# A graph aggregation kernel: the run gathers, the leftover gathers and the start of the last merge block are put at other places in the program

## The chip, the core and the metric

One core of one Trainium2 chip runs the whole kernel. The metric is the device time of one execution in microseconds. Before the change it is 1911.4 us, the median of three runs (1903.02, 1911.40 and 1920.62).

## The reference

Every one of 12500 nodes adds up the feature rows of its neighbours over 800000 edges, scales the sum and applies two small weight matrices.

```
N, deg, D = 12500, 64, 64
E = N * deg
def reference(x, src, dst, deg_inv, w_self, w_neigh):
    nsum = _segment_sum(x[src], dst, N)
    h_neigh = nsum * deg_inv[:, None]
    return x @ w_self + h_neigh @ w_neigh
```

`src` and `dst` are drawn at random, so what is costly is the gather `x[src]` and the sum by `dst`.

## The kernel before

**Sorting.** Each edge becomes a key that holds its bucket: 78 groups of 160 destination nodes, times 98 blocks of 128 source nodes, which is 7644 buckets of some 105 edges. VectorE sorts 128 rows of 6250 keys each by compare and exchange (lines L229). The sorted rows are then cut into pieces ("runs") so that one partition gets a run from every row, and the runs of one partition are merged. This is done in two parts: part 0 holds buckets 0 to 4735 (128 partitions of 37), part 1 the rest (128 of 23). GpSimd (POOL) fetches the runs with one indirect DMA for each of the 128 runs of a part (`gather_runs`, line L393), and after each of them writes a small tile once or twice (`pause`, L306). VectorE merges them (`merge_runs`, L415 for the first step of a block of runs and L455 for the others).

**Windows.** In the merged rows each bucket has a window. A count over the row finds where it begins, and POOL fetches it with an indirect DMA (`find_and_gather`, tile `v`, L605). The windows of part 0 come in two halves: the lower buckets, whose rows are merged first, and the upper ones. `decode_buckets` takes the windows apart: destination numbers are turned on TensorE and kept in `dlT`, source numbers go to DRAM as `sl`. Edges that do not fit a window become "leftovers" (`leftovers`), 64 columns of up to 128 edges for each part.

**Sums.** `nodes` walks over the buckets in tiles of eight: 956 tiles, numbered from 0. For each group of 28 buckets (three and a half tiles) SyncE loads `slb`, and VectorE makes the one-hot matrices `ohs` (L823) and `ohd` (L826); there are three buffers for `ohs`, so VectorE can be about ten tiles ahead. For each tile TensorE multiplies the one-hots with the node features (L852 into `ct`, eight matmuls), ScalarE copies `ct` to `xg` (L862), and TensorE adds `xg` times `ohd` into the sums `acc` (L907, sixteen matmuls). Six groups of destinations share one pair of accumulators, so a stretch ends after 588 buckets, which is 73.5 tiles. ("Octet" is the code's word for such a stretch: `OCT`.)

**Leftovers in the sums.** `uses` gives every leftover column the bucket number from which it may be added: the moment of its use. `rest` is called at every tile. At most five columns ahead of use it lets POOL gather the 128 feature rows of a column by an indirect DMA (tile `lx`, L871), then VectorE makes its one-hot (`ohl`, L879), and at the use TensorE multiplies the two (L887). TensorE takes its instructions in order, so it stands still at L887 until the gather has landed.

**Who sets the order.** The order on each engine is written out by hand (`manual_schedule`): the merge of part 1 is a generator from which some steps are taken at every tile. Its first block (runs 0 to 63) runs beside the windows of part 0; its second block (64 to 95) from tile 8 on; its third block (96 to 127) and all that follows from tile `RESUME` on. POOL's run gathers for part 1 stand in three places: 64 behind the row search, 32 behind the upper windows, and the last 32, one at each odd tile, from tile 1 to tile 63. POOL, like every engine, works its instructions off in order.

Of the kernel before, what the change touches and what calls it, by code (L numbers as in the profile page):

```python
# [22 lines left out]
NB = 98  # L23
# [21 lines left out]
EDGE = 32  # L45
PAUSE = (1, 2)
FIRST = 64
THEN = 96
EXT = 31
SIDE = H + EXT  # L50
# [3 lines left out]
BIG = float(np.array(BIGBITS, np.uint32).view(np.float32))  # L54
SIG = 5.5
AHEAD = 44
RESUME = 80
PACE = 420
SHARE = 503
SHARED = 60  # L60
# [9 lines left out]
OCT = 6  # L70
# [190 lines left out]
class Kernel:  # L261
# [533 lines left out]
    def uses(self):  # L795


        out = []
        for o in range(0, NBID, OCT * NB):
            end = min(o + OCT * NB, NBID)  # L800
            here = []
            for p in range(2):
                for c in range(64):
                    lo = max(o, BASE[p] + c * 2 * KPRS[p])
                    hi = min(end, BASE[p] + (c + 1) * 2 * KPRS[p])
                    if hi > lo:
                        here.append([max(hi + 56, 380 + 24 * c) if p == 0 else hi + 56, p, c, lo // NB, (hi - 1) // NB])
            at = end + 8
            for use in sorted(here)[::-1]:
                at = use[0] = min(use[0], at - 24)  # L810
            out += sorted(here)
        return out
# [16 lines left out]
    def nodes(self, pool, aps, mps):  # L829
# [34 lines left out]

        def rest(b0):

            if len(picked) < self.used + 5 and len(picked) < len(uses) and uses[len(picked)][0] - 160 <= b0 \
                    and uses[len(picked)][1] in self.left:
                _, p, c, _, _ = uses[len(picked)]
                x = pool.tile([128, 128], FH, name="lx", bufs=5)  # L870
                nc.gpsimd.indirect_dma_start(  # L871
                    out=x, out_offset=None, in_=self.xt,
                    in_offset=bass.IndirectOffsetOnAxis(ap=self.left[p][1][:, c:c + 1], axis=0))
                picked.append(x)
                self.picked = len(done)
            if len(ohl) < len(picked) and len(ohl) < self.used + 5 and uses[len(ohl)][0] - 96 <= b0:
                _, p, c, first, end = uses[len(ohl)]
                m = pool.tile([128, 4 * HN], FH, name="ohl", bufs=5)
                nc.vector.tensor_scalar(m[:, :(end + 1 - first) * 2 * HN], self.wide[:, :(end + 1 - first) * 2 * HN],  # L879
                                        self.left[p][0][:, c:c + 1], -float(first * 2 * HN),  # L880
                                        op0=OP.subtract, op1=OP.is_equal)
                ohl.append(m)
            while self.used < len(uses) and uses[self.used][0] <= b0:
                _, p, c, first, end = uses[self.used]
                m = ohl[self.used].rearrange("p (b h n) -> p b h n", h=2, n=HN)
                for h in range(2):
                    nc.tensor.matmul(acc[h][:, first % OCT * HN:(first % OCT + end + 1 - first) * HN],  # L887
                                     picked[self.used], m[:, :end + 1 - first, h], start=False, stop=False)
                self.used += 1
# [167 lines left out]
    def after_sort(self, es, mps, aps):  # L1057
        tc = self.tc
        l2, l2b, l2a, va = ExitStack(), ExitStack(), ExitStack(), ExitStack()
        self.merged = self.lower = False  # L1060


        with tc.manual_schedule():
            low, middle, high = self.segments
            sync = tc.nc.sync
            for step in low:
                step()
            sync.dma_start(self.d1[0][:, :SPLITS[0]], self.runs[:, :SPLITS[0]])
            rows = self.find_rows(0, mps)
            n = 0  # L1070
            for i, step in enumerate(middle):
                step()
                while n < NEARLY * (i + 1) // len(middle):
                    n = next(rows) + 1
            sync.dma_start(self.d1[0][:, SPLITS[0]:SPLITS[1]], self.runs[:, SPLITS[0]:SPLITS[1]])
            u1, other, u0 = [stack.enter_context(tc.tile_pool(name=f"l2{i}", bufs=1))
                             .tile([128, 2 * EDGE + 128 * WIDE[p]], F32, name="u")
                             for i, (stack, p) in enumerate(((l2, 1), (l2b, 0), (l2a, 0)))]
            for u in (u1, other, u0):
                tc.nc.gpsimd.memset(u[:, :EDGE], 0.0)  # L1080
            for _ in rows:
                pass
            self.gather_runs(0, u0, range(128))
            for step in high:
                step()
            sync.dma_start(self.d1[1], self.runs[:, UPPER1:])
            self.l1ab.close()
            rows = self.find_rows(1, mps)
            for _ in range(SHARED):
                next(rows)  # L1090
            ways = None
            for i, _ in enumerate(self.merge_runs(0, u0, other, ((0, 2), (2, 1), (3, 1)))):
                if rows and [next(rows, None) for _ in range(2 - i % 2)][-1] is None:
                    rows = None
                    self.l1b.close()
                    self.gather_runs(1, u1, range(FIRST))
                    dl = es.enter_context(tc.tile_pool(name="dl", bufs=1, side="right"))
                    self.dlT = dl.tile([128, NCOL], BF, name="dlT")
                if self.lower and not ways:
                    vp = va.enter_context(tc.tile_pool(name="va", bufs=1, side="right"))  # L1100
                    self.windows(0, vp)
                    self.store_rows(0, sync)
                    ways = self.find_and_gather(0, range(NLOWER), 1)
                elif ways and i % 2:
                    next(ways, None)
            for _ in ways:
                pass
            self.store_rows(1, sync)
            self.sums_and_merge(es, mps, aps, u1, other, l2, l2b, l2a, va, vp)

    def sums_and_merge(self, es, mps, aps, u1, other, l2, l2b, l2a, va, vp):
# [11 lines left out]
        for slot in range(at[-1] + 2):  # L1123
            t += SLOT
            if ways and next(ways, None) is None:
                ways = None
                self.gather_runs(1, u1, range(FIRST, THEN))
            if slot < KPRS[0] - NLOWER and not on_act2(0, NLOWER + slot):
                t -= 750
            if slot in at or slot - 1 in at:  # L1130
                next(decode)
                t -= 1175
            while t > 0 and steps < per:
                t -= next(merge)
                steps += 1
# [11 lines left out]
        for n in self.nodes(fin, aps, mps):  # L1147
            if left and n >= left_at:
                wait = next(left, None)
                if wait is None:  # L1150
                    left = None
                    if 1 in self.left:
                        self.check(fin, mps)
                else:
                    left_at = n + wait
            if runs and n % 2:
                self.gather_runs(1, u1, [runs.pop(0)])
            if tail and n % 2:
                next(tail, None)
            if merge and n >= 8 and (n >= RESUME or steps < 2 * per):  # L1160
                t += PACE
                while merge and t > 0:
                    dt = next(merge, None)
                    steps += 1
                    if dt is None:
                        merge = None
                        self.merged = True
                        assert self.rows is u1
                        l2b.close()
                        vp = vb.enter_context(tc.tile_pool(name="vb", bufs=1))  # L1170
                        self.windows(1, vp)
                        self.store_rows(2, tc.nc.scalar)
                        find = self.find_and_gather(1, range(KPRS[1]), LAG)
                    else:
                        t -= dt
            elif find:
                if n % 2 == 0 and self.picked < n - 1 and next(find, None) is None:
                    find = None
                    decode = self.decode_buckets(1, self.v, vp, mps)
                    tail = self.tail(mps)  # L1180
            elif decode:
                if next(decode, None) is None:
                    assert n < 128 * KPRS[0] // 8 - 12
                    decode = None
                    left, left_at = self.leftovers(1, mps), 0
# [29 lines left out]
```

## Time and profile before

| what | value |
|---|---|
| median of three runs | 1911.4 us |
| time of the profiled execution | 1896.69 us |
| its span, first to last instruction | 1895.0 us |
| VectorE (DVE) busy | 1677.9 us, 89% |
| ScalarE (ACT) busy | 1166.8 us, 62% |
| TensorE (PE) busy | 962.2 us, 51% |
| GpSimd (POOL) busy | 841.8 us, 44% |
| mean granted TensorE clock | 0.793 |

The shares are averages over stages that have different limits: the first 800 us sort and merge on VectorE, with TensorE almost idle, and the sums fill the rest. So the table only says where to look; what a change in one stage is worth has to be read from that stage.

### The profile page before, as it was taken

The page shows a single profiled execution, that of the slowest core. Times are in us where ns is not written, and L with a number is a line of the kernel's source. Part 1 is how long each engine was busy: PE and PEld are TensorE (multiplying, and loading weights), DVE is VectorE, ACT ScalarE, POOL GpSimd, SP SyncE. Part 2 cuts the span into 40 slices and gives each one's busy share as a digit, 9 for nine tenths or more (in the row PEclk, how much of TensorE's full clock was granted, in tenths as well). Part 3 has the DMA queues.
Part 4 walks back from the last instruction along what each step waited for, and adds up shares of the span by engine and source line. Part 5 has one row for each costly group of instructions (what it writes and reads, how often), then busy time and mean ns, then how long its engine had stood idle before and what let it go on. Part 6 is the DMA issues. An engine that isn't in the chain of part 4 may idle for free.

```text
span 1895.0 us, 54521 instructions
## 1 busy us (share of the span) xinstructions
PE 962.2 (51%) x23659; PEld 838.7 (44%) x23659; DVE 1677.9 (89%) x1778; ACT 1166.8 (62%) x1835; POOL 841.8 (44%) x917
## 2 busy tenths in 40 slices
PE   0033000000000000083788887988979999889987
PEld 0023000000000000073677776777768788778886
DVE  7999999997749999795699999998998898888885
ACT  7463019305510022574689888988988887788786
POOL 1000000599889984798737322204662232322421
PEclk9985555555555555587899999999999999999998
DMA  4322000001100012274577877779867888888874
GB/s 152 70 63 73 0 24 8 25 20 52 22 20 10 10 38 70 82 283 137 185 230 246 256 244 251 251 258 312 285 223 250 270 276 257 269 272 278 272 252 147
DMA packets 104804, 305.24 MB, mean 161 GB/s; under 512 B 52945, under 2 KB 60491, under 8 KB 103915
## 3 DMA queue, kind: packets, MB, share of 16 engines
q1 hardware_dynamic: 86347, 277.44, 41.5%
q0 software_dynamic: 17632, 22.17, 8.7%
q8 instruction: 187, 3.06, 0.6%
q10 hardware_dynamic: 576, 2.07, 0.3%
q14 instruction: 62, 0.51, 0.1%
HBM read 282.20 MB, written 19.41 MB: 159 GB/s over the span
## 4 chain that ended last, share of the span: by engine, by line
DVE 40%; PE 24%; POOL 18%; issue 11%; DMA 3%; ACT 3%; DVEq 0%; SPq 0%; ACTq 0%; POOLq 0%
DVE u L455 14%; PE ct L852 13%; POOL u L393 13%; PE acc L907 9%; DVE a L229 7%; DVE b L229 7%; DVE ohd L826 5%; DVE ohs L823 4%; POOL pad L306 3%; POOL lx L871 2%; ACT xg L862 2%; DMA slb<-sl 1%; PE po L970 1%; DMA rd<-dst 1%; PE acc L887 1%
## 5 line engine op out<-in xcount | busy, mean ns | idle before, releaser
L862 ACT ACTIVATE xg<-ct 128x1024 f16<-128x1024 f32 (+1 forms) x898 | 856.4, 1043 | 188.6 <-PE ct L852 167.1
L852 PE MATMUL ct<-xh,ohs 128*128 128x128 f16 x7644 | 540.3, 224 | 69.7 <-DVE ohs L823 36.2
L852 PEld LDWEIGHTS <-ohs 128*128 128x128 f16 x7644 | 449.4, 100 | 110.0 <-issue 51.3
L393 POOL DMA_INDIRECT u<-d,ix x256 | 369.4, 1443 | 217.0 <-DVE ix L385 175.3
L907 PE MATMUL acc<-ohd,xg 64*128 64x80 f16 x15288 | 399.9, 200 | 58.9 <-issue 40.5
L455 DVE TENSOR_TENSOR u<-u 128x1456 f32<-128x1456 f32 (+46 forms) x292 | 394.5, 1378 | 6.6
L871 POOL DMA_INDIRECT lx<-xt,lsrc x140 | 265.6, 1897 | 249.1 <-PE acc L887 213.1
L907 PEld LDWEIGHTS <-xg 64*128 64x128 f16 x15288 | 318.4, 96 | 126.2 <-issue 57.4
L826 DVE TENSOR_TENSOR ohd<-iota,dlT 128x2240 f16<-128x2240 bf16 x273 | 360.3, 1320 | 0.0
L823 DVE TENSOR_SCALAR ohs<-slb,pidx 128x3584 f16<-128x3584 bf16 x273 | 314.6, 1152 | 37.4 <-PE ct L852 25.7
L383 PE MATMUL stp<-idf,st 128*128 128x128 f32 x2 | 0.9, 446 | 356.7 <-DVE st L381 356.7
L229 DVE TENSOR_TENSOR a<-b 128x608 f32<-128x608 f32 (+44 forms) x124 | 173.9, 1445 | 4.6
L229 DVE TENSOR_TENSOR b<-a 128x608 f32<-128x608 f32 (+44 forms) x124 | 173.9, 1444 | 4.3
L978 POOL DMA_DIRECT2D out<-o x25 | 22.8, 913 | 319.7 <-DVE o L977 245.5
L383 PEld LDWEIGHTS stp<-idf,st 128*128 128x128 f32 x2 | 0.4, 182 | 357.2 <-issue 357.2
L662 PE MATMUL tr<-idb,l 128*128 128x128 bf16 x60 | 8.0, 273 | 262.2 <-ACT l L656 258.1
L860 DVE CAST xg<-ct 128x1024 f16<-128x1024 f32 x64 | 78.3, 1223 | 57.6 <-PE ct L852 57.1
L662 PEld LDWEIGHTS <-l 128*128 128x128 bf16 x60 | 5.0, 117 | 265.5 <-ACT l L656 260.8
L420 ACT ACTIVATE u<-u 128x30 f32<-128x30 f32 (+34 forms) x136 | 30.7, 278 | 134.8 <-DVE u L455 73.0
L231 ACT ACTIVATE b<-a 128x1 f32<-128x1 f32 (+21 forms) x52 | 18.7, 379 | 135.5 <-DVE a L229 130.4
L605 POOL DMA_INDIRECT v<-d,ix x60 | 75.4, 1257 | 59.6 <-ACT ix L623 47.4
L374 ACT ACTIVATE junka<-b,c 128x132 bf16<-128x132 f32 (+46 forms) x205 | 90.6, 442 | 11.8 <-DVE b L229 5.9
(153 smaller groups left out, 798.6 us busy)
## 6 DMA issues: line engine op xcount, KB each, us to landing
slb<-sl SPq DMA_DIRECT2D x273, 896.0 KB
u<-d,ix POOLq DMA_INDIRECT x256
xt<-xh SPq DMA_DIRECT2D x1, 3136.0 KB
fo<-own SPq DMA_DIRECT2D x26, 120.0 KB
own<-os SPq DMA_DIRECT2D x12, 256.0 KB
out<-o POOLq DMA_DIRECT2D x24, 120.0 KB
lx<-xt,lsrc POOLq DMA_INDIRECT x140
rd<-dst SPq DMA_DIRECT2D x4, 521.0 KB
```

Source lines behind the costliest of these rows:

```text
L229: nc.vector.tensor_tensor(view(dst, lo + sh, [[st, g], [1, l]]), x, y, op=op)
L374: nc.scalar.activation(junks[0][:, :n], w, AF.Sign, bias=self.c1[:, 0, c:c + 1], accum_out=a)
L393: nc.gpsimd.indirect_dma_start(out=u[:nr, EDGE + p * w:EDGE + (p + 1) * w], out_offset=None, in_=src, in_offset=bass.IndirectOffsetOnAxis( ...
L455: nc.vector.tensor_tensor(view(dst, EDGE + o + out, d), view(src, EDGE + o + x, d), view(src, EDGE + o + x + gap, d), op=op)
L605: self.nc.gpsimd.indirect_dma_start(out=self.v[:, k].bitcast(F32), out_offset=None, in_=flat(self.d2[home(part, k)], 128 * PITCH2[home(par ...
L823: nc.vector.tensor_scalar(s.rearrange("p c s -> p (c s)"), b, self.pidx[:, :1], None, op0=OP.is_equal)
L826: nc.vector.tensor_tensor(d, self.iota[:, None].to_broadcast([128, 14, HN, 2]), ix, op=OP.is_equal)
L852: nc.tensor.matmul(ct[:, i * 128:(i + 1) * 128], cols[i][0], self.xh[:, (b0 + i) % NB].rearrange("p a f -> p (a f)"), start=True, stop=True)
L860: nc.vector.tensor_copy(xg[:, :cnt * 128], ct[:, :cnt * 128])
L862: nc.scalar.activation(xg[:, :cnt * 128], ct[:, :cnt * 128], AF.Copy)
L871: nc.gpsimd.indirect_dma_start(out=x, out_offset=None, in_=self.xt, in_offset=bass.IndirectOffsetOnAxis(ap=self.left[p][1][:, c:c + 1], ax ...
L907: nc.tensor.matmul(acc[h][:, db % OCT * HN:(db % OCT + 1) * HN], xg[r, i * 128:(i + 1) * 128], d[r], start=db % OCT == 0 and sb == 0, stop ...
```

## The change

Five numbers or rules are changed. The amount of work stays the same: 128 run gathers for part 1, 140 leftover gathers, the same merge steps.

1. Runs 64 to 70 of part 1 are gathered behind the windows of the lower buckets, ahead of the upper windows, and no longer behind them (`MORE = 71`).
2. The last 32 runs are issued at every third tile, from tile 0 to tile 93.
3. The third block of the merge begins at tile 100, not 80 (`RESUME`).
4. In the first stretch the eight leftover columns are all due at its end, 24 buckets apart: from bucket 404 on (404, 428, ..., 572), where the old rule set the first at 380.
5. In that stretch a column's gather may be issued up to 400 buckets ahead of its use, and no longer 160.

```
-RESUME = 80
+MORE = 71
+RESUME = 100
 ...
-                        here.append([max(hi + 56, 380 + 24 * c) if p == 0 else hi + 56, p, c, lo // NB, (hi - 1) // NB])
+                        here.append([end if o == 0 else hi + 56, p, c, lo // NB, (hi - 1) // NB])
 ...
-            if len(picked) < self.used + 5 and len(picked) < len(uses) and uses[len(picked)][0] - 160 <= b0 \
+            early = 400 if b0 < OCT * NB - 160 else 160
+            if len(picked) < self.used + 5 and len(picked) < len(uses) and uses[len(picked)][0] - early <= b0 \
 ...
+            self.gather_runs(1, u1, range(FIRST, MORE))
             self.store_rows(1, sync)
 ...
-                self.gather_runs(1, u1, range(FIRST, THEN))
+                self.gather_runs(1, u1, range(MORE, THEN))
 ...
-            if runs and n % 2:
+            if runs and n % 3 == 0:
                 self.gather_runs(1, u1, [runs.pop(0)])
```

**POOL, between the lower and the upper windows of part 0.** `v` are window gathers (18 lower, 19 upper), `u` a run gather of part 1, `pad` its pause. Before:

```order
L393 DMA u<-d_1_61,ix_1468 128x48
L306 MEMSET pad 128x95 x2
L605 DMA v<-d_0_64,ix_0_1803 128x190 x18
L605 DMA v<-d_1_65,ix_0_1803 128x190 x19
L393 DMA u<-d_1_61,ix_1468 128x48
L306 MEMSET pad 128x95 x2
```

After:

```order
L606 DMA v<-d_0_64,ix_0_1803 128x190 x18
L394 DMA u<-d_1_61,ix_1468 128x48
L307 MEMSET pad 128x95 x2
...
L606 DMA v<-d_1_65,ix_0_1803 128x190 x19
L394 DMA u<-d_1_61,ix_1468 128x48
L307 MEMSET pad 128x95 x2
```

Seven of the pairs `u`, `pad` now stand between the two groups of windows (the pairs left out at the dots are the other six).

**POOL, in the first stretch of the sums.** `lx` is a leftover gather. Before, the first one stands behind 47 run gathers that follow the upper windows, and the next ones are mixed with run gathers:

```order
L871 DMA lx<-xt,lsrc_2726 128x128
L393 DMA u<-d_1_61,ix_1468 128x48
L306 MEMSET pad 128x95 x2
L871 DMA lx<-xt,lsrc_2726 128x128
L393 DMA u<-d_1_61,ix_1468 128x48
L306 MEMSET pad 128x95 x2
L393 DMA u<-d_1_61,ix_1468 128x48
```

After, five of them stand close together behind 30 run gathers, and the sixth and seventh behind twelve more:

```order
L873 DMA lx<-xt,lsrc_2723 128x128 x2
L394 DMA u<-d_1_61,ix_1468 128x48
L307 MEMSET pad 128x95 x2
L873 DMA lx<-xt,lsrc_2723 128x128 x2
L394 DMA u<-d_1_61,ix_1468 128x48
L307 MEMSET pad 128x95 x2
L873 DMA lx<-xt,lsrc_2723 128x128
L394 DMA u<-d_1_61,ix_1468 128x48
L307 MEMSET pad 128x95 x2
...
L873 DMA lx<-xt,lsrc_2723 128x128 x2
```

So the first five columns are issued 17 run gathers sooner, while the sixth column (due at bucket 524) has 44 run gathers and five `lx` ahead of it. Behind it come two run gathers, two `lx`, four runs, `lx`, three runs, `lx`, two runs, an output, a run, `lx`, and run 127, the last.

**VectorE, where the third block of the merge begins.** `u<-u` with 16x41 is the first step of the block. Before, it follows the second block at once:

```order
L455 TENSOR_TENSOR u<-u 128x441
L455 TENSOR_TENSOR u<-u 128x429
L415 TENSOR_TENSOR u<-u 128x16x41
L823 TENSOR_SCALAR ohs<-slb,pidx 128x3584
L826 TENSOR_TENSOR ohd<-iota,dlT 128x2240
L415 TENSOR_TENSOR u<-u 128x16x41
```

After, only one-hots stand ahead of it:

```order
L881 TENSOR_SCALAR ohl<-wide,lp_2721 128x320
L824 TENSOR_SCALAR ohs<-slb,pidx 128x3584
L827 TENSOR_TENSOR ohd<-iota,dlT 128x2240
...
L416 TENSOR_TENSOR u<-u 128x16x41
L881 TENSOR_SCALAR ohl<-wide,lp_2721 128x320
L416 TENSOR_TENSOR u<-u 128x16x41
```

Counted in groups of one-hots, the block's first step has moved from behind the 26th to behind the 31st, which is from tile 84 to tile 100, and the steps after it, the search of the windows of part 1 and their decoding by four groups, 14 tiles.

## The prediction

> **What bounds the kernel now.** I read the busy times by slice first:
>
> ```profile
> span 1895.0 us, 54521 instructions
> PE   0033000000000000083788887988979999889987
> DVE  7999999997749999795699999998998898888885
> ```
>
> A slice is 47.4 us. The sums begin in the 18th; in the next one and the one after TensorE (PE) falls to 3 and 7, and VectorE (DVE) to 5 and 6: something holds up both. PE's waits name it (time in all, times, longest):
>
> ```profile
> PE acc L887 <- DMA lx<-xt,lsrc: 37.6, 4, 26.5
> ```
>
> Next PE's timeline (start, duration; in brackets the idle time before and its releaser), then DVE's:
>
> ```profile
> 891.13 0.32 PE L887 MATMUL acc<-ohl,lx 128*128 128x80 f16 x2 [26.53 <-DMA lx<-xt,lsrc]
> 903.30 0.45 PE L887 MATMUL acc<-ohl,lx 128*128 128x160 f16 x2 [5.03 <-DMA lx<-xt,lsrc]
> 919.46 0.45 PE L887 MATMUL acc<-ohl,lx 128*128 128x160 f16 x2 [5.83 <-DMA lx<-xt,lsrc]
> 891.48 0.30 DVE L879 TENSOR_SCALAR ohl<-wide,lp 128x320 f16<-128x320 f16 x1 [21.43 <-PE acc L887]
> 906.78 1.15 DVE L823 TENSOR_SCALAR ohs<-slb,pidx 128x3584 f16<-128x3584 bf16 x1 [6.00 <-PE ct L852]
> 921.56 1.39 DVE L823 TENSOR_SCALAR ohs<-slb,pidx 128x3584 f16<-128x3584 bf16 x1 [6.96 <-PE ct L852]
> 941.68 1.39 DVE L415 TENSOR_TENSOR u<-u 128x656 f32<-128x656 f32 x1 [1.09 <-issue]
> ```
>
> PE waits for the first leftover column from 864.6 to 891.1, and twice again; DVE runs its buffers full and stops too. The last row is the third merge block. POOL's timeline shows why `lx` is late:
>
> ```profile
> 733.34 0.95 POOL L605 DMA_INDIRECT v<-d,ix  x1 [0.30 <-issue]
> 753.63 0.98 POOL L605 DMA_INDIRECT v<-d,ix  x1 [19.34 <-ACT ix L623]
> 785.76 0.94 POOL L393 DMA_INDIRECT u<-d,ix  x1 [0.30 <-issue]
> 834.55 2.94 POOL L393 DMA_INDIRECT u<-d,ix  x1 [0.15 <-issue]
> 838.07 2.92 POOL L393 DMA_INDIRECT u<-d,ix  x1 [0.16 <-issue]
> 856.65 1.35 POOL L393 DMA_INDIRECT u<-d,ix  x1 [0.15 <-issue]
> 871.62 0.95 POOL L393 DMA_INDIRECT u<-d,ix  x1 [0.15 <-issue]
> 887.74 0.95 POOL L871 DMA_INDIRECT lx<-xt,lsrc  x1 [0.96 <-issue]
> 935.18 1.63 POOL L393 DMA_INDIRECT u<-d,ix  x1 [0.30 <-issue]
> ```
>
> From 785.76 on POOL has no idle time to speak of. Its run gathers (L393 by window, count in brackets) set the pace:
>
> ```profile
> 640.00:703.00 63.00, 49.02 (x25) 0.50 0.08 23
> 830.00:853.00 23.00, 18.93 (x8) 1.00 0.72 258
> 853.00:870.00 17.00, 12.44 (x8) 0.92 0.73 259
> 870.00:887.00 17.00, 10.44 (x11) 0.50 0.14 40
> ```
>
> With its pause, a gather takes 2.9 us, then 2.1, and 1.55 while DVE stands still. So POOL is the bound up to 935.18, where run 127 is issued and the third block may follow. After it DVE is full for 346 us, up to the last merge step, and then the sums run at the pace of PE and ScalarE. Busy times of all engines in the first row (PE, PEld, DVE, ACT, POOL), of L907 alone in the others:
>
> ```profile
> 1200.00:1250.00 50.00, 42.10 (x1128) 36.87 (x1126) 49.97 (x46) 43.63 (x48) 12.25 (x9) 1.00 0.78 247
> 827.00:863.60 36.60, 15.61 (x576) 12.31 (x576) 0.96 0.74 263
> 941.70:1287.60 345.90, 128.84 (x5024) 102.64 (x5024) 0.99 0.79 248
> 1450.00:1850.00 400.00, 160.24 (x6200) 127.81 (x6200) 0.98 0.84 269
> ```
>
> DVE is busy 49.97 of 50 us. A tile has 16 of these matmuls, so 576, 5024 and 6200 make 36, 314 and 387.5 tiles: 1.02 us a tile before the stall, 1.10 in the merge, 1.03 at the end.
>
> **The change, part by part.** The time is worked out from two things: the moment X at which the third block starts (941.68 now), and the tile at which it starts.
>
> *Seven gathers ahead of the upper windows.* They fall into the idle 19.34 us that end at 753.63. Beside a merging DVE 25 gathers took 63 us, 2.52 each, so seven take 17.6: hidden, with 1.7 us left. Without that cover (2.9 each) they take 20.2 and push the upper windows by 1 us. I take 0. They shorten POOL's list behind 785.76 by seven gathers.
>
> *The first five columns.* Thirty run gathers stand ahead, not 47. The 31st gather was issued at 856.65; that is where the first `lx` goes now. Its use is at tile 51, three tiles behind the tile at which PE stopped, at 864.6 + 3 × 1.02 = 867.7. From issue to PE took 3.4 us (887.74 to 891.13), so it is there at 860. The fifth follows four `lx` and two gathers later, about 869, and is due at 877 to 878. No stall; both ends of the pace below leave this so, except the slowest, where the fifth is just late.
>
> *The sixth column, due at tile 66.* Five `lx` at 1.9 us (no pause behind them) and two gathers at 2.1 bring POOL to 856.65 + 9.5 + 4.2 = 870.4. Then come twelve gathers. PE gets to tile 66 at 863.6 + 18 × 1.02 = 882 and waits; DVE goes on for some 5 us, as it did before (PE stopped at 864.6, DVE at 891.48 − 21.43 = 870.05). So up to 887 POOL does 16.6 / 2.1 = 7.9 gathers, the other 4.1 at 1.55 take 6.4, and the sixth `lx` is issued at 893.4. PE goes on at 896.8: a stall of 15 us, where there were 37.6. The seventh is issued right behind, the eighth two gathers later; both are in time.
>
> *Run 127 and X.* Behind the sixth `lx` twenty more instructions lead to run 127, itself among them. For a mix of gathers, `lx` and pauses beside a working DVE 1.9 us each lies between 1.55 and 2.1: 894.7 + 19 × 1.9 = 931 for its issue. It took 941.68 − 935.18 = 6.5 us at most from there to the merge step, 3.4 at least for a quick landing, so X = 937, where I take 6. DVE itself comes to this place when PE is at tile 95 or 96, 896.8 + 29.5 × 1.02 = 927, and waits 10 us; its one-hots last PE nearly as long. Between tiles 86 and 100 DVE has only one-hots to make,
>
> ```profile
> L826 DVE TENSOR_TENSOR ohd<-iota,dlT 128x2240 f16<-128x2240 bf16 x273 | 360.3, 1320 | 0.0
> L823 DVE TENSOR_SCALAR ohs<-slb,pidx 128x3584 f16<-128x3584 bf16 x273 | 314.6, 1152 | 37.4 <-PE ct L852 25.7
> ```
>
> 2.47 us for 3.5 tiles or 0.71 a tile, so 0.3 × 14 = 4 us of DVE go unused there, the price of `RESUME = 100`; it lies inside the wait for X.
>
> *What follows.* From X to the end of the merge is DVE work of the same length, 346 us, but it ends 14 to 15 tiles further on, so the last stage has 14.5 tiles less: 14.5 × 1.03 = 15 us. Part 1 is ready 14 tiles later; its last transposes come at tile 508 in place of 494, and it is wanted from bucket 4736, tile 592: 80 tiles cover that, and its price is 0.
>
> **Sum.** Span 1895 − (941.7 − 937) − 15 = 1875.3 us. The profiled execution took 1896.69 us, 1.7 more than its span; the median of the runs shown is 1911.4, so this execution was a quick one. Scaled by 1911.4 / 1895 the forecast is 1891.5 us, 1.0% faster. X is the open cost: 930 (DVE hardly waits) with 16 tiles saved gives a span of 1867, or 1883 us; the slowest POOL is the third rival. The runs before differ by 0.9%, so about 1% is what can be told from no change.
>
> **Rivals.**
>
> *The stall is gone altogether* (1871 us). POOL would have to keep 1.55 us a gather: run 127 near 913, X 917, span 1855. The window 870 to 887 shows the pace, but only with DVE at rest; windows with DVE at work speak against it.
>
> *The stall moves and most is given back* (1904 us). At 2.6 us a gather the sixth `lx` lands near 901, X is 950, span 1888. The average before the stall is close to this: 30 gathers from 785.76 to 856.65, 2.4 us each. Against it, the last eight before DVE stopped took 2.1.
>
> *POOL is held by VectorE for its whole list: slower* (1925 us). From 834.55 to 838.07 a gather took 3.5 us, just the length of a round of DVE's work at that place:
>
> ```profile
> 832.70 1.15 DVE L823 TENSOR_SCALAR ohs<-slb,pidx 128x3584 f16<-128x3584 bf16 x1
> 836.22 1.15 DVE L823 TENSOR_SCALAR ohs<-slb,pidx 128x3584 f16<-128x3584 bf16 x1
> ```
>
> Today's long stall lets POOL catch up (11 gathers in 17 us); with less stall DVE works on and POOL pays for it. At 3.5 a gather and 3 an `lx`, with the catch-up while DVE stands, the sixth `lx` is issued at 902 and X is 971: span 1895 + 29 − 15 = 1909. The change turns into a loss once X passes 957. Against it: the same DVE work let eight gathers through in 17 us at 853 to 870. The Trainium skill bears on this ("SBUF — State Buffer", section "Who interferes with whom"): a VectorE instruction in a two-port mode locks GpSimd out for its whole length, so that GpSimd cannot write descriptors. By this rule the rival is what a busy VectorE brings; the trace agrees in direction, 0.95 us for an issue beside an idle DVE against 2.94 beside a busy one, but not with 1.35 at 856.65, where DVE was as busy (its idle time begins at 870.05).
>
> **How the numbers follow.** The forecast has 0.56; X between 930 and 945 puts it at 1883 to 1900 us, 0.33 faster by over 1%, 0.23 within. The stall gone: 0.12, faster. Given back: 0.13, within 1%. Slower: 0.19, of which 0.06 within 1% and 0.13 beyond, since with the upper windows late as well its price comes to the 1% mark. Together faster 0.45, same 0.42, slower 0.13. The range goes from 1870, the price of the first rival, to 1922, near that of the third.
>
> **What would show it.** In the changed profile: run gathers in the idle time before 753; the first `lx` near 857; no wait at L887 before tile 66 and one of 10 to 20 us there, near 882; the third block's first step at 930 to 945 with DVE idle some 10 us before it; the merge's last step some 5 us sooner, with more tiles done by then. A wait at the first column, a third block behind 957, or a late first upper window would prove me wrong.

## The result and the profile after

The change makes the kernel about half a per cent faster: 1902.62 us in the median of 20 runs (1890.45 to 1914.36), against 1912.88 us for the kernel before (20 runs, 1901.9 to 1920.62). The medians differ by 10.3 us. The ratio is 0.994, with a 95% interval of 0.9919 to 0.9961, which is a gain between 7.5 and 15.5 us. The forecast was 1891.5 us, some 20 us faster. The sign was right, and about half of the size came.

The profiled execution of the changed kernel took 1913.5 us. It is among the slowest of its 20, so its span can't be set against the 1895.0 of before; what can be compared is each stage. First the busy times by slice (47.8 us each):

```profile
span 1911.8 us, 54520 instructions
PE   0043000000000000185888898788878989888987
DVE  6999999997749999796799999998896878788985
```

Where the slices 18 to 20 had 8, 3 and 7 for PE, they now have 8, 5 and 8, and DVE has 6 and 7 for 5 and 6 in the last two: the hole at the beginning of the sums is smaller. PE's waits for a leftover column have gone from 37.6 us in four to a single one:

```profile
PE acc L889 <- DMA lx<-xt,lsrc: 13.4, 1, 13.4
```

POOL's timeline (start, duration; in brackets the idle time before and its releaser) shows the seven run gathers ahead of the upper windows, then the upper windows, the run gathers behind them, the first and the sixth `lx`, an output transfer and run 127:

```profile
735.30 2.01 POOL L394 DMA_INDIRECT u<-d,ix  x1 [0.30 <-issue]
750.81 1.01 POOL L394 DMA_INDIRECT u<-d,ix  x1 [0.16 <-issue]
754.45 0.98 POOL L606 DMA_INDIRECT v<-d,ix  x1 [2.20 <-ACT ix L624]
785.75 0.94 POOL L394 DMA_INDIRECT u<-d,ix  x1 [0.30 <-issue]
856.80 2.12 POOL L873 DMA_INDIRECT lx<-xt,lsrc  x1 [0.96 <-DVE ohl L881]
894.97 0.95 POOL L873 DMA_INDIRECT lx<-xt,lsrc  x1 [0.53 <-issue]
932.79 1.38 POOL L980 DMA_DIRECT2D out<-o  x1 [10.78 <-DVE ohl L881]
939.59 1.83 POOL L394 DMA_INDIRECT u<-d,ix  x1 [0.30 <-issue]
```

The upper windows begin 0.8 us later than before (754.45 for 753.63) and still wait 2.20 us for ScalarE, and the run gathers behind them begin at 785.75 for 785.76: the seven are hidden. The sixth `lx`, at 894.97, is the one PE waits for, and behind it comes the third block. PE's row at the sixth column, DVE's at the first step of the third block (X), and DVE's first search of a window of part 1, which marks the end of the merge:

```profile
898.08 0.45 PE L889 MATMUL acc<-ohl,lx 128*128 128x160 f16 x2 [13.36 <-DMA lx<-xt,lsrc]
946.20 1.29 DVE L416 TENSOR_TENSOR u<-u 128x656 f32<-128x656 f32 x1 [4.36 <-DMA lx<-xt,lsrc]
1290.59 0.32 DVE L602 TENSOR_SCALAR_CACHE_REDUCE junk<-u,c 128x114 bf16<-128x114 f32 x1
```

X was 941.68 before, and the merge ended at 1287.63. This execution is thus some 3 us *later* at the end of the merge, with some 14 tiles more done. Its long time has another reason, in the last stage. L909 alone (which was L907), in the same 400 us as in the prediction:

```profile
1450.00:1850.00 400.00, 155.29 (x5912) 123.07 (x5912) 0.97 0.82 261
```

These are 369.5 tiles, 1.08 us a tile, where the profiled execution of before did 387.5, 1.03 us a tile. The next experiments tell whether that belongs to the change.

### The profile page after: what moved, and what is told of

Same layout as the page of the kernel before. It is cut to its first block, busy times and chain, and to the rows that moved or that the text cites. A ratio compares the mean times of both kernels' runs of the same rounds, so it can differ in the third digit from the quotient of the medians.

```text
span 1911.8 us, 54520 instructions
## 1 busy us (share of the span) xinstructions
PE 983.8 (51%) x23659; PEld 850.9 (45%) x23659; DVE 1678.6 (88%) x1778; ACT 1168.6 (61%) x1835; POOL 808.2 (42%) x917
## 4 chain that ended last, share of the span: by engine, by line
DVE 40%; PE 25%; issue 13%; POOL 12%; ACT 4%; DMA 4%; DVEq 0%; SPq 0%; ACTq 0%; POOLq 0%
PE ct L853 14%; DVE u L456 14%; PE acc L909 10%; POOL u L394 9%; DVE a L230 7%; DVE b L230 7%; DVE ohd L827 5%; DVE ohs L824 4%; ACT xg L863 2%; POOL pad L307 2%; DMA slb<-sl 1%; POOL lx L873 1%; DMA rd<-dst 1%; PE acc L889 1%; PE po L972 1%
## 5 line engine op out<-in xcount | busy, mean ns | idle before, releaser
L853 PE MATMUL ct<-xh,ohs 128*128 128x128 f16 x7644 | 549.7, 224 | 78.5 <-DVE ohs L824 33.1
L394 POOL DMA_INDIRECT u<-d,ix x256 | 372.1, 1453 | 218.4 <-DVE ix L386 175.3
L909 PE MATMUL acc<-ohd,xg 64*128 64x80 f16 x15288 | 409.3, 200 | 76.6 <-issue 57.5
L909 PEld LDWEIGHTS <-xg 64*128 64x128 f16 x15288 | 322.6, 96 | 148.9 <-issue 77.9
L873 POOL DMA_INDIRECT lx<-xt,lsrc x140 | 229.0, 1636 | 270.3 <-PE acc L889 236.9
```

The source lines that it names most:

```text
L394: nc.gpsimd.indirect_dma_start(out=u[:nr, EDGE + p * w:EDGE + (p + 1) * w], out_offset=None, in_=src, in_offset=bass.IndirectOffsetOnAxis( ...
L853: nc.tensor.matmul(ct[:, i * 128:(i + 1) * 128], cols[i][0], self.xh[:, (b0 + i) % NB].rearrange("p a f -> p (a f)"), start=True, stop=True)
L873: nc.gpsimd.indirect_dma_start(out=x, out_offset=None, in_=self.xt, in_offset=bass.IndirectOffsetOnAxis(ap=self.left[p][1][:, c:c + 1], ax ...
L909: nc.tensor.matmul(acc[h][:, db % OCT * HN:(db % OCT + 1) * HN], xg[r, i * 128:(i + 1) * 128], d[r], start=db % OCT == 0 and sb == 0, stop ...
```

## Experiments

They ran in three sets, each beside runs of the kernel before on its own chip (medians 1906.4, 1903.9 and 1911.2 us); the first two sets had the same chip, the third another. Each kernel ran 12 times, e7 6, e8 9 and e10 11 times. All ratios are against the kernel before in the same set. "End of the merge" is the first search of part 1, as above; the three columns in us come from one profiled execution each. X alone does not set the time: e7 and e8 differ by 11.8 us in the median, and their intervals do not meet, with X 0.9 us apart.

| kernel | X (us) | end of merge (us) | PE waits for `lx` (us) | ratio [95%] |
|---|---|---|---|---|
| before | 941.7 | 1287.6 | 37.6 | 1 |
| e1_again (the change) | 938.8 | 1283.2 | 15.0 | 0.9945 [0.9907, 0.9983] |
| e2_eight | 940.5 | 1284.9 | 11.1 | 0.9996 [0.9967, 1.0026] |
| e3_out_later | 938.8 | 1282.8 | 13.7 | 0.9927 [0.9898, 0.9957] |
| e4_columns | 940.4 | 1286.3 | 42.2 | 0.9950 [0.9919, 0.9980] |
| e5_seven | 929.6 | 1275.6 | 27.8 | 0.9939 [0.9916, 0.9963] |
| e6_resume | 950.9 | 1294.9 | 26.8 | 1.0025 [0.9995, 1.0055] |
| e7_nopause | 920.8 | 1265.2 | 0 | 0.9864 [0.9830, 0.9898] |
| e8_all | 921.7 | 1265.8 | 0 | 0.9927 [0.9901, 0.9954] |
| e9_share | 938.9 | 1283.3 | 10.7 | 0.9942 [0.9916, 0.9967] |
| e10_best | 944.4 | 1288.9 | 0 | 0.9931 [0.9901, 0.9960] |
| e11_resume80 | 936.0 | 1281.9 | 33.9 | 0.9949 [0.9926, 0.9971] |
| e12_nopause80 | 927.8 | 1273.6 | 0 | 0.9949 [0.9918, 0.9979] |

### The change once more, and its output transfer

e1_again is the changed kernel without an edit.

> The changed kernel unaltered, for a second profile. The first one showed the third merge block starting at X = 946.2, because POOL waited 10.8 us at an output DMA ahead of run 126, and a tensor engine that lost some 7 us in issue gaps of 0.5 us between 903 and 922. Theory A (end of the kernel = before + (X - 941.7) - 15 us for 14.5 tiles fewer in the last stage, with X set by POOL's list): ratio to before 0.994 (0.991 to 0.997). If the issue gaps belong to that one execution, the wait at the output DMA is under 5 us here and X is 936 to 941; if the output DMA always holds POOL, X is 944 to 948 again.

e3_out_later puts the output transfers of the first stretch ten tiles later, behind run 127 on POOL:

```
-late.append([b0 + 40 * (1 + 3 * q), ...
+late.append([b0 + 40 * (1 + 3 * q) + (80 if o == 0 else 0), ...
```

> The changed kernel with the output steps of the first stretch ten tiles later, so that their DMAs stand behind run 127 in POOL's list. Theory A: POOL no longer waits there, run 127 is issued 8 to 10 us sooner (about 930), X is 935 to 938, and the time is some 8 us less than the changed kernel's, ratio to before 0.990. Rival R: the wait at tile 66 stays 13 us, so the time stays, ratio 0.994.

Measured: 0.9945 for the change, 0.9927 with the outputs later, so no difference that can be told, and X is 938.8 in both. In the second execution of the change, DVE's start of the third block, its first search, and PE's wait (all of e1_again):

```profile
938.84 1.29 DVE L416 TENSOR_TENSOR u<-u 128x656 f32<-128x656 f32 x1 [5.74 <-DMA u<-d,ix]
1283.22 0.32 DVE L602 TENSOR_SCALAR_CACHE_REDUCE junk<-u,c 128x114 bf16<-128x114 f32 x1
898.51 0.45 PE L889 MATMUL acc<-ohl,lx 128*128 128x160 f16 x2 [15.04 <-DMA lx<-xt,lsrc]
930.84 1.34 POOL L980 DMA_DIRECT2D out<-o  x1 [0.48 <-issue]
```

The stall is 15.0 us and X is 938.84, close to the forecast of 15 and 937. The last row is the output transfer: it waited 0.48 us here, 10.78 in the first profile, where POOL came to it sooner (at 922.0, here at 930.4). So the long wait does not belong to every execution of the change; it comes back in e7 and e10 (9.46 and 12.66 us). This execution took 1889.22 us.

### Is the wait at the sixth column worth its 15 us?

e2_eight gives `lx` three buffers more, so that all eight columns of the first stretch can be gathered ahead:

```
-if len(picked) < self.used + 5 and ...
+if len(picked) < max(8, self.used + 5) and ...
-x = pool.tile([128, 128], FH, name="lx", bufs=5)
+x = pool.tile([128, 128], FH, name="lx", bufs=8)
```

> The changed kernel with eight lx buffers in place of five, and all eight leftover columns of the first stretch gathered early. Both theories: no wait for a leftover gather at tile 66. Theory A: POOL has as many gathers ahead of run 127 as before and loses the time in which VectorE stood still, so X stays within 5 us of the changed kernel's, VectorE waits longer at the third block, and the time is within 5 us of the changed kernel (ratio to before 0.992 to 0.997). Rival R (each microsecond of wait at a leftover counts as such): 13 us less than the changed kernel, ratio to before 0.987.

The wait at tile 66 is gone, but PE stands a little later, at the first column that did not fit into the eight:

```profile
915.42 0.31 PE L889 MATMUL acc<-ohl,lx 128*128 128x80 f16 x2 [11.14 <-DMA lx<-xt,lsrc]
940.52 1.29 DVE L416 TENSOR_TENSOR u<-u 128x656 f32<-128x656 f32 x1 [9.12 <-DMA u<-d,ix]
```

X stays at 940.52, and DVE's wait for it has grown to 9.12 us. Here the stall of PE is only where POOL's lateness shows; lifting it in one place moved it to the next. The ratio, 0.9996, is some 10 us worse than the change's, where the end of the merge differs by 1.7. Its profile took 624.5 us from there to the end, e1's 604.3; why, was not found.

### The parts alone

e5_seven has only the seven gathers:

```
+MORE = 71
+            self.gather_runs(1, u1, range(FIRST, MORE))
-                self.gather_runs(1, u1, range(FIRST, THEN))
+                self.gather_runs(1, u1, range(MORE, THEN))
```

> The kernel before with the seven gathers alone. Theory A (POOL's list of gathers sets the start X of the third merge block, and the end follows as 1 us per us of X and about 1.03 us per tile that is done ahead of it): 40 gathers instead of 47 stand ahead of the first leftover column, which is issued some 11 to 16 us sooner (872 to 877 instead of 887.7), PE's long wait there falls from 26.5 to 10 to 16 us, X falls by 7 gathers at 1.55 to 2.1 us, to 927 to 931, the tile at which it starts stays; ratio 0.992 to 0.995. Theory B (what counts is only how many tiles are ahead of the block, PE and ScalarE being the bound of the whole): X falls, but the tiles ahead of it stay, ratio 0.998 to 1.002.

The first step of the third block, and PE's waits from 800 to 1000:

```profile
929.65 1.37 DVE L416 TENSOR_TENSOR u<-u 128x656 f32<-128x656 f32 x1 [1.11 <-issue]
```

```profile
PE acc L888 <- DMA lx<-xt,lsrc: 27.8, 7, 15.8
```

X came 12.0 us sooner, the merge ended 12.1 us sooner, and the median fell by 11.8 us (1892.1 against 1903.85). Here the time moved as far as X (by the interval of the ratio, 7 to 16 us), and this part alone gives as much as the whole change.

e4_columns has only the two lines on the leftover columns, with the run gathers and the third block where they were:

```
-here.append([max(hi + 56, 380 + 24 * c) if p == 0 else hi + 56, p, c, ...
+here.append([end if o == 0 else hi + 56, p, c, ...
-... uses[len(picked)][0] - 160 <= b0
+early = 400 if b0 < OCT * NB - 160 else 160
+... uses[len(picked)][0] - early <= b0
```

> The kernel before with the leftover columns' part of the change alone (first use at bucket 404, gathers up to 400 buckets ahead); seven gathers, last runs and third block as before. Both: no wait at the first column. Theory A: 59 run gathers stand ahead of the sixth column, so PE waits some 35 us at tile 66; run 127 is issued about 931, X is about 937 at tile 84 as before: 0 to 5 us faster, ratio 0.997 to 1.000. Rival P (the columns alone bring the change's gain): ratio 0.994.

```profile
PE acc L888 <- DMA lx<-xt,lsrc: 42.2, 3, 27.2
```

PE's waits (800 to 1000 us) are longer than before, not shorter, and X and the end of the merge differ from before by 1.3 us. All the same the ratio is 0.995. The lower end of that gain, 0.2% or 4 us, is near what X gives, the middle is not; this one stays open. A gain of half a per cent can thus come without the mechanism of the prediction, so that e5's agreement supports it and does not prove it.

e6_resume has only the later third block and every third tile for the last runs:

```
-RESUME = 80
+RESUME = 100
-            if runs and n % 2:
+            if runs and n % 3 == 0:
```

> The kernel before with the later third block and every third tile for the last runs, nothing else. Theory A: the wait at the first column stays at 26 us, the two shorter ones shrink, DVE comes to the block at about 950, X 945 to 955 with 14 tiles more ahead of it: span 3 to 13 minus 15, ratio 0.994 to 0.999. Theory B: the tiles ahead of the block count whole, ratio 0.990 to 0.993.

X is 950.86, as far out as theory A put it, the merge ends 7.3 us later than before, and the kernel is not faster: the ratio is 1.0025, with 1 just inside its interval (1908.7 against 1903.85, 4.9 us). By the prediction's arithmetic 15 tiles ahead would have turned this into 8 us of gain. e11_resume80 is the counterpart, the change without these two edits:

> The seven gathers and the column change, but the third block from tile 80 and every second tile for the last runs as before. If the tiles put ahead of the third block are worth nothing at the end (they are given back behind the merge), only X counts: X 925 to 931 with 14 to 15 tiles fewer ahead of it, ratio 0.992 to 0.995, the same as the change or better. If the tiles are worth 1.03 us each, this comes out 5 to 8 us above the change, ratio 0.997 to 1.000.

At 0.9949 it can't be told from the change. So the later block brings nothing that can be measured, alone or with the rest. Its X is 936.0, not the 925 to 931 that both theories took: with a run gather at every second tile, eighteen instead of twelve stand ahead of the sixth `lx`, and PE waits there in full,

```profile
917.00 0.45 PE L889 MATMUL acc<-ohl,lx 128*128 128x160 f16 x2 [27.53 <-DMA lx<-xt,lsrc]
```

which is the moved stall of the prediction's second rival, in a kernel in which the columns come early without the thinner run gathers. It did not cost e11 its gain.

### Where fifteen tiles go

Behind the merge, what counts is how many tiles are left. L907 (L908 or L909 in the others) counted in two stretches, from the end of the merge to the end, and from 80 to 200 us behind it; before first, then the change (e1_again):

```profile
1287.63:1895.00 607.37, 234.17 (x8962) 186.28 (x8960) 0.96 0.80 259
1367.63:1487.63 120.00, 42.06 (x1594) 33.80 (x1592) 0.94 0.73 243
```

```profile
1283.22:1887.50 604.28, 229.08 (x8716) 181.47 (x8710) 0.95 0.78 253
1363.22:1483.22 120.00, 38.41 (x1400) 31.07 (x1400) 0.86 0.64 212
```

At 16 a tile, 560 tiles are left before and 545 after, as was forecast, but they take 607 and 604 us. In the second row of each is the reason: in these 120 us the kernel before does 99.6 tiles, the change 87.5. In the seven profiles with the block at tile 100 and `SHARE` untouched it is 84.5 to 91.5, in the five with it at tile 80, 99.6 to 102.5, whatever X is. e5 and e6, for the two kinds:

```profile
1355.55:1475.55 120.00, 42.38 (x1640) 33.77 (x1632) 0.97 0.74 243
```

```profile
1374.89:1494.89 120.00, 36.13 (x1353) 29.26 (x1355) 0.89 0.64 208
```

In this stretch VectorE searches part 1's windows and takes them apart; it is busy 54.8 of the first 60 of these 120 us in e1. From tile 503 (`SHARE`) on it also takes conversions of `ct` to `xg` from ScalarE. That number did not move with the block, so the conversions begin 14 to 15 tiles sooner in part 1's work. From the end of the merge to the flag that closes part 1 (groups by line; count, busy time, mean, idle before), before and then e1_again:

```profile
L860 DVE CAST xg<-ct 128x1024 f16<-128x1024 f32 x2 | 2.4, 1221 | 0.0
```

```profile
L861 DVE CAST xg<-ct 128x1024 f16<-128x1024 f32 x4 | 4.9, 1214 | 1.7 <-PE ct L853 1.7
```

There is also a wait of VectorE (e1_again) for a small transfer that POOL issues shortly ahead; in the kernel before no such wait shows.

```profile
DVE ts L758 <- DMA tk<-d: 7.4, 1, 7.4
```

e9_share moves `SHARE` along:

```
-SHARE = 503
+SHARE = 518
```

> The change with SHARE at 518 instead of 503, so that VectorE begins to take over conversions of xg as many tiles behind the end of the merge as in the kernel before. Where the third block starts later by 14 to 15 tiles, the last stage did not get shorter: from 80 to 200 us behind the end of the merge it did 84 to 89 tiles, against 101 to 104. Theory D (VectorE gets the conversions while it is still the bound with part 1's windows, and TensorE waits for them): 2 conversions ahead of the flag in place of 4, no wait of TensorE for xg at a gather there, 94 to 102 tiles in that stretch, the time 4 to 10 us below the change's, ratio 0.989 to 0.993. Theory E (something else in that stretch takes the tiles back, for one the wait for tk of 6 to 7 us): 84 to 90 tiles, ratio 0.993 to 0.997.

The same group, the same wait and the same 120 us in e9:

```profile
L861 DVE CAST xg<-ct 128x1024 f16<-128x1024 f32 x2 | 2.4, 1216 | 0.0
```

```profile
DVE ts L758 <- DMA tk<-d: 3.7, 1, 3.7
```

```profile
1363.30:1483.30 120.00, 42.29 (x1548) 33.35 (x1544) 0.91 0.70 225
```

The wait for `tk` does not explain the tiles: it is 2.5 us in the first profile of the change and 2.4 in e3, less than e9's 3.7, with 87.5 and 91.5 tiles done. What sets the kernels apart is how long TensorE waits for VectorE in these 120 us, for `xg` and `ohs` together: 12.3 to 14.6 us in the seven profiles named above, 5.5 at most in the other seven (e9 3.3, e10 2.7). The rows of e1 and then of the kernel before:

```profile
PE ct L853 <- DVE xg L861: 5.1, 2, 2.8
PE ct L853 <- DVE ohs L824: 4.2, 1, 4.2
PE acc L909 <- DVE xg L861: 4.2, 1, 4.2
```

```profile
PE acc L907 <- DVE xg L860: 5.0, 3, 4.6
```

The trace does what theory D says: two conversions, 96.8 tiles, three quarters of the loss back. The time does not: 0.9942, the change's own ratio. e10_best, with the same edit, did 96.5 tiles in that stretch. So the conversions are shown to be what slows this stretch, but that they are what the change's median lacks is not shown: of the nine tiles that e9 wins there on e1, half had been lost in the 80 us ahead (71.8 tiles for 76.3), and the other half goes in the 400 us behind, where e9 does 376 tiles in 405 us, e1 381 in 404, before 387 in 407. Single executions differ there by as much, so what sets that pace stays open.

### POOL's list without its pauses

e7_nopause leaves out the small tile that POOL writes behind each run gather of part 1 (two writes of 0.23 us on the mean, in the row of L307 below):

```
-PAUSE = (1, 2)
+PAUSE = (1, 0)
```

> The change with POOL's pause (0.58 us behind each gather of part 1) left out. Theory A: the 56 gathers, seven of them hidden anyway, reach run 127 some 25 us sooner, no wait at tile 66, DVE goes from column to column and X is its own arrival, 912 to 922; span 17 to 25 us shorter than the change's, ratio 0.980 to 0.987 against the kernel before. Theory C (a gather beside a working DVE takes DVE's round, 3.5 us, whatever stands behind it): the pace stays at 2.9 to 3.5, X 935 to 945, ratio as the change's 0.993 to 0.996.

Two groups of POOL from 785 to 860, of e1_again and then of e7, and e7's X:

```profile
L394 POOL DMA_INDIRECT u<-d,ix x30 | 49.9, 1663 | 4.8 <-issue 4.8
L307 POOL MEMSET pad<- 128x95 f32 x60 | 14.0, 233 | 1.7
```

```profile
L394 POOL DMA_INDIRECT u<-d,ix x41 | 55.1, 1343 | 12.5 <-issue 12.5
```

```profile
920.79 1.30 DVE L416 TENSOR_TENSOR u<-u 128x656 f32<-128x656 f32 x1 [2.38 <-DMA u<-d,ix]
```

Without the pauses POOL issues 41 run gathers and five `lx` in 75 us, in place of 30 and two. No wait for `lx` is left, X is 18 us sooner than the change's, the merge ends 18 us sooner, and the ratio is 0.9864: 1877.84 us, 26 us below the kernel before and the fastest of all. This also settles the third rival. From 830 to 880 VectorE is busy 49.90 of 50 us in both kernels; L394 there, of e1 and then of e7:

```profile
830.00:880.00 50.00, 30.03 (x14) 1.00 0.77 257
```

```profile
830.00:880.00 50.00, 26.42 (x18) 0.99 0.79 255
```

An issue takes 2.15 us on the mean with the pauses and 1.47 without them, not a round of 3.5 us. In the prediction that rival stood beside a page of the Trainium skill ("SBUF — State Buffer", section "Who interferes with whom"), by which VectorE in a two-port mode shuts GpSimd out for an instruction's length; single issues of 1.6 to 2.9 us fit such a hold, a whole list held at that pace was not seen.

e8_all adds the eight buffers and the later outputs (later by ten tiles, as in e3, and not by two as its expectation says):

> As e7_nopause, with eight lx buffers issued ahead and the output transfers of the first bucket group put two tiles later. Theory A: nothing waits for POOL any more, X 910 to 918, ratio 0.978 to 0.985, at most 4 us below e7_nopause. Theory C: as the change, 0.993 to 1.000.

It got X = 921.7 and 0.9927: no more than e7, and less. Run 127 was issued at 899.99 here, 15 us sooner than in e7 (914.90), and X stayed where it was, with no wait of VectorE ahead of it: without the pauses VectorE's own arrival sets X, and no longer POOL. Like e2, the other kernel with eight buffers, it lost time behind X, where its one profile took 616 us from the end of the merge, against 604 to 614 for the others of the first two sets with the block at tile 100, e2 aside; how the buffers would do that was not found. In the third set, on another chip, two kernels without pauses were tried, with the moved `SHARE` (e10_best) and with the block at tile 80 and a run gather at every second tile (e12_nopause80):

> The change without POOL's pause and with SHARE at 518. Theory D: the gains add, 24 to 32 us below the kernel before and some, ratio 0.980 to 0.984. Theory E: as without the pause alone, 0.984 to 0.989.

> As e11_resume80, without POOL's pause. Tiles worth nothing: X 905 to 914 at tile 84, ratio 0.981 to 0.986, at or below the change without the pause (0.986). Tiles worth 1.03 us each: 6 to 10 us above that, 0.988 to 0.992.

Both missed, at 0.9931 and 0.9949. In e10, X is 944.4 although POOL has no pause and PE no wait for `lx`. PE's waits from 830 to 880 in e7 and then in e10 (in all, times, longest), with L909's matmuls there:

```profile
PE ct L853 <- ACT xg L863: 4.7, 3, 2.1
PE acc L909 <- issue: 1.5, 2, 1.0
PE ct L853 <- issue: 0.8, 1, 0.8
```

```profile
830.00:880.00 50.00, 19.72 (x736) 15.45 (x736) 0.99 0.79 255
```

```profile
PE acc L909 <- issue: 8.9, 15, 1.2
PE ct L853 <- issue: 4.5, 7, 2.4
```

```profile
830.00:880.00 50.00, 16.98 (x524) 12.04 (x519) 0.80 0.52 172
```

PE stood 13.4 us in 22 pieces in which it waited for nothing that the profile shows, and did 33 tiles in place of 46. The granted clock did not begin it: it is 1.00 from 838 to 842, when the row of gaps in this stretch begins, and falls to 0.50 from 846 to 862, while PE stands. PE came to the first leftover column at 885.76, in e7 at 865.54, and POOL stood for the buffer that this frees:

```profile
886.27 1.53 POOL L873 DMA_INDIRECT lx<-xt,lsrc  x1 [26.26 <-PE acc L889]
```

In e7 that wait is 1.18 us. In the same 50 us PE stood without a visible wait for 18.0 us in e12, and for 0.7 in e9, with the pauses and on the same chip. So on that chip a good part of what the missing pauses save is lost to PE standing still. Whether denser gathers cause that was not tried with anything else held fixed, and the comparison with e7 is one between chips.

## Why the prediction was right, and where it was not

*Seven gathers hidden, price 0: right.* The upper windows were 0.8 us late and the gathers behind them not at all. e5 shows what it brings: X 12 us sooner, and alone as much gain as the whole change.

*First five columns: right.* The first `lx` was issued at 856.80, where 856.65 was forecast, and no column ahead of tile 66 waits.

*Sixth column: right.* `lx` at 894.97 for 893.4, a stall of 13.4 and 15.0 us for 15.

*X = 937: right in the number* (938.8 in e1 and e3, 938.9 in e9), *and in e1 by luck*. There run 127 was issued at 936.16, where 931 was forecast, and the block followed 2.7 us later instead of 6: two errors that cancel. In e9 (931.60, and 7.3 us) both terms hold. VectorE came to the block at 933 to 937 in these three, by X less its wait, and not at 927. In the first profile X is 9 us late. The output transfer ahead of run 126 on POOL, a term I had put at nothing, waited 10.78 us there, and run 127 was issued at 939.59. Since the transfer waits 0.48 us in e1 and 0.47 in e9, and moving it (e3) changes nothing that can be told, the term is mostly 0 in the change.

*"14.5 tiles less × 1.03 = 15 us": this is the step that failed.* The tiles are ahead, 545 left for 560. But the nine profiles with the block at tile 100 take 604 to 625 us from the end of the merge, 612 on the mean, and the five with it at tile 80 607 to 624, 616 on the mean. Not 15 us but 3 came, less than the profiles scatter. I had priced "part 1 later by 14 tiles" at 0, since 80 tiles cover its being *ready*. That is not where it costs: the work itself came to lie against a number, `SHARE`, that stays at its tile, and VectorE had more to do in a stretch in which it is nearly full and TensorE waits for it (13.5 us in e1, 5.0 before). e9 shows that by the trace; what of it is in the time, it doesn't show. With 3 for 15, and e1's 4.4 us at the end of the merge, the sum is 7.5 us, against the 10.3 measured.

*The scaling* from one execution to the median (1911.4 / 1895) did no harm here, but the changed kernel's two profiled executions took 1913.5 and 1889.2 us; one span is no measure for changes of 10 us.

*The rivals.* The stall does not go altogether (13.4 us are left), it does when the pauses go. The stall moves in e2 and e11, but only in e2 is the gain given back (0.9996, against 0.9949). POOL held at 3.5 us a gather did not happen: X was 939 to 946, not 971.

## What to carry to other kernels

Ask of a late gather what stands ahead of it on its queue, and move that into the queue's idle time: seven gathers that cost nothing where they went gave as much alone as the whole change, and lifting the wait itself only moved it. When one stage is moved against another that counts in its own units (tiles, buckets), look for every constant written in those units; a tile that is done sooner is only worth its time if the stage behind is not made slower by what now coincides. Take the end of a stage in two or three executions before pricing a few microseconds from it.

## What the runs showed of the hardware

PE can stand without any wait that the profile shows: in the first profile of the change, every 0.75 us for some 0.5 us,

```profile
905.25 0.26 PE L909 MATMUL acc<-ohd,xg 64*128 64x80 f16 x4 [0.48 <-issue]
906.01 0.25 PE L909 MATMUL acc<-ohd,xg 64*128 64x80 f16 x4 [0.50 <-issue]
906.76 0.27 PE L909 MATMUL acc<-ohd,xg 64*128 64x80 f16 x4 [0.50 <-issue]
```

four matmuls at a time. In e1 there are 1.4 us of such gaps between 880 and 930, in the first profile of the change 6.9, in e10 13.4 between 830 and 880. What PE lacks then is not shown.

Beside a VectorE busy for 49.90 of 50 us, a POOL issue took 2.15 us on the mean with two small writes behind each run gather (e1) and 1.47 without (e7); beside an idle one it took 0.95. Leaving those writes out brought X 18 us sooner on one chip.

A higher mean granted clock did not mean a shorter time. The mean was 0.974 in the first profile of the change and 0.793 in that of the kernel before, and the two differ above all in the sort, where TensorE is almost idle (0.9 against 0.5 in the slices there). Of the 34 executions of the kernel before in the third set, 13 had a mean near 0.97 and a median time of 1911.95 us, 21 had one near 0.80 and 1911.05 us.
